# A converted weight's sign as a 16-bit half on GpSimd, and the decay of the scan's state on VectorE

## The chip, the cores and the metric

One Trainium2 chip, one core of it. The metric is the device time of one execution in microseconds (us). Engines are named as in the profile: PE is TensorE's matmul and PEld its weight load, DVE is VectorE, ACT is ScalarE, POOL is GpSimd, SP is SyncE, which issues nearly all the DMAs here. Every engine has its own queue and takes its instructions in order: an instruction that waits for a semaphore holds up all that stand behind it on that engine.

## The reference, cut to what matters

A recurrent attention over 768 steps for 4 batches of 8 heads (head size 40) gives 3072 rows of 320, and two feed-forward blocks follow.

```
for t in range(S):
    y[:, :, t] = einsum('bhd,bhde->bhe', rt, state)
    Sa = einsum('bhde,bhe->bhd', state, at)
    state = state * wt[:, :, None, :] - einsum('bhd,bhe->bhde', Sa, bt) \
            + einsum('bhd,bhe->bhde', vt, kt)
h = x @ w_in;  x1 = (max(h, 0) + alpha * min(h, 0)) @ w_out      # d_ff 2048
g = x1 @ w_gate;  out = (silu(g) * (x1 @ w_val)) @ w_out         # d_ff 1536
```

The weights of both feed-forward blocks lie in memory as 64-bit floats and have to be made 32-bit floats by the kernel itself.

## The kernel before, in words

**The scan.** The steps are worked in chunks of 64, two chunks to an item, and 24 items (six blocks of 128 steps, m = 0 to 5, times 4 batches). `preps` makes the decay products of an item by scans on DVE and scales its inputs; `inverse(m)` inverts the 64 x 64 triangular systems of the whole block m by a chain of some 100 small DVE operations (a product into `tmp`, L645, and a subtraction from `la`, L653, for 31 columns), then two block transposes (L656, L658), from which PE takes the block `eps` (L666); `seq` runs an item's two chunks one after the other: `zp` (PE, L749), `zs` (ACT), `pp` (PE), `ut` (ACT), transposes of `ut` and of the state (PE, L767 and L771), `gp` (PE), the mask (DVE, L785), `yp` (PE), the sum into the state `ST` (DVE, L805) and the output `pv` (DVE, L809). Between two chunks `enter_chunk` multiplies the state by its decay three times: for the two halves of the next chunk's operand `gs` (DVE, 64 x 160 each, L726), and in place for the whole state (POOL, 128 x 160, the same line). POOL also copies `v` into the other halves of `gs` (L740) and makes the triangular selections of `AN` (L598).

**The weights.** `conv1` turns the 32 tiles (128 x 384 and 128 x 320 by turns) of the first block's two matrices into pairs of 32-bit parts, a rounded one and the rest, and writes them to memory as `wd`, from where the first block's matmuls fetch them again (`wt`). Of a 64-bit weight, `narrow` makes a 32-bit one in four passes: ACT scales the upper word, which leaves exponent and upper mantissa in `wz` (L191); ACT brings the upper 16 bits of the lower word to their place in `wy` (L192); DVE puts the sign bit of the upper word into `wy` (L193); DVE shifts `wz` by 3 and joins `wy` (L194). Then ACT rounds (`wc`, L218) and POOL subtracts (`wc`, L219). There are two buffers of `raw`, `wz` and `wc` and one of `wy`. The second block's weights go another way, `gated`, which the change leaves alone; its POOL comparison of one input (L213) serves below as a price.

**The order.** The program is written in generators that `drive` interleaves by shares and priorities, and a list scheduler of the compiler orders each engine's instructions from that. So a changed line moves other instructions too. `inverse(0)` runs beside the first weight tiles; `seq` of block 0, the preparation of block 1 and `inverse(1)` run beside the rest of them; from then on the first feed-forward block's matmuls of block m run beside the scan of block m + 1. The last part is the second feed-forward block alone.

Of the kernel before, what the change touches and what calls it, by code (L numbers as in the profile page):

```python
# [10 lines left out]
U16 = mybir.dt.uint16  # L11
ACTF = mybir.ActivationFunctionType
ALU = mybir.AluOpType
# [60 lines left out]
def kernel(  # L74
# [15 lines left out]
    nc = tc.nc  # L90
# [94 lines left out]
    def narrow(pool, raw):  # L185
        whi, wlo = raw[..., 1], raw.bitcast(U16)[..., 1]
        sh = list(whi.shape)
        y = pool.tile(sh, U32, tag="wy", name="wy", bufs=YB)
        z = pool.tile(sh, U32, tag="wz", name="wz", bufs=ZB)
        f = z.bitcast(F32)  # L190
        nc.scalar.activation(out=f, in_=whi.bitcast(F32), func=ACTF.Copy, scale=2.0 ** -112)  # L191
        nc.scalar.activation(out=y, in_=wlo, func=ACTF.Copy, scale=2.0 ** -13, bias=2.0 ** -14 - 0.5)  # L192
        nc.vector.scalar_tensor_tensor(y, whi, 0x80000000, y, ALU.bitwise_and, ALU.bitwise_or)  # L193
        nc.vector.scalar_tensor_tensor(z, z, 3, y, ALU.logical_shift_left, ALU.bitwise_or)  # L194
        return f

# [24 lines left out]
    def conv(stage, idx, src, f, kind, into=None, dve=0):  # L221
        sw = words(src)
        if kind == "up":
            raw = stage.tile([128, 3, 128, 2], U32, tag="raw", name="raw", bufs=RB)
            sw = sw[:, f * 128:f * 128 + 128]
            nc.sync.dma_start(out=raw[:, 0:2], in_=sw[0:256].rearrange("(j p) n two -> p j n two", p=128))
            for p in (lo, hi):
                nc.sync.dma_start(out=raw[p, 2], in_=sw[256:DM])
        else:
            raw = stage.tile([128, DM, 2], U32, tag="raw", name="raw", bufs=RB)  # L230
            nc.sync.dma_start(out=raw, in_=sw[f * 128:f * 128 + 128])
        w32 = narrow(stage, raw) if idx < 2 * K1 else gated(stage, raw, dve)
        t = stage.tile([128, 768], F32R, tag="wc", name="wc", bufs=WCB) if into is None else into
        if kind == "up":
            t3 = t.rearrange("p (a b) -> p a b", a=6)
            split(w32, t3[:, 0:3], t3[:, 3:6], nc.gpsimd)
        elif kind == "down":
            split(w32[:, 0:256], t[:, 0:256], t[:, 256:512], nc.gpsimd)
            split(w32[:, 256:DM], t[:, 512:512 + RT], t[:, 512 + RT:2 * DM], nc.gpsimd)
        else:  # L240
            split(w32, t[:, 0:DM], t[:, DM:2 * DM], nc.gpsimd)
        if into is None:
            n = 768 if kind == "up" else 2 * DM
            nc.sync.dma_start(out=wd[idx, :, 0:n], in_=t[:, 0:n].bitcast(F32))
# [186 lines left out]
    raw = {}  # L431
    for j, pool in ((0, rawp), (1, bp)):
        for nm in ("w", "bk"):
            sh = [128, 2, NP, TB] if nm == "bk" else [128, 1, NP, TB]
# [267 lines left out]
    def seq(i, ch, own=None):  # L702
# [19 lines left out]
        std = st[:, :, 0:D].rearrange("q (a j) d -> q a j d", j=2)  # L722

        def decayed(eng, out, pr, c):
            wc = wv_all[pr, :, :, c, L:L + 1].to_broadcast([pr.stop - pr.start, NP // 2, 2, D])
            eng.tensor_tensor(out=out, in0=std[pr], in1=wc, op=ALU.mult)  # L726

        def enter_chunk(c):
            t = gs_p.tile([128, NP, 2, L + D], F32, tag="gs", name="gs")
            for h, pr in ((0, lo), (1, hi)):  # L730
                decayed(nc.vector, t[pr, h::2, :, L:L + D], pr, c)
            decayed(nc.gpsimd, std, slice(0, 128), c)
            return t

        nxt = enter_chunk(0)
        for c in range(CPB):
            cs = slice(c * L, c * L + L)
            gs = nxt
            for h, pr in ((0, hi), (1, lo)):
                nc.gpsimd.tensor_copy(  # L740
                    out=gs[pr, h::2, :, L:L + D],
                    in_=rv.rearrange("t (q j d) -> t q j d", j=2, d=D)[(lo, hi)[c], h::2],
# [11 lines left out]
            for q in range(NP):  # L754
                for j, pr in ((0, lo), (1, hi)):
                    u = q // 2 * 2 + j
                    n = bb * NSEG + slots[u][1] * CPB + c
# [14 lines left out]
            for h, pr in ((0, lo), (1, hi)):  # L772
                nc.scalar.mul(
                    out=gs[pr, h::2, :, L:L + D],
                    in_=pp[pr, 1].rearrange("p (a j) d -> p a j d", j=2)[:, :, :, 0:D], mul=-1.0,
# [5 lines left out]
            for q in range(NP):  # L781
# [4 lines left out]
                out=gs[:, :, :, 0:L].rearrange("q p h t -> q (p h) t"),  # L786
# [5 lines left out]
            for u, p in slots:  # L792
                s = p * CPB + c
                u0, j = u // 2 * 2, u % 2
# [11 lines left out]
            if c < CPB - 1:  # L806
                nxt = enter_chunk(c + 1)
            wv = wv_all[:, :, :, c, :]
            nc.vector.tensor_tensor(  # L809
                out=xo.rearrange("q (j a) c t -> q a j c t", j=2)[:, :, :, c],  # L810
# [303 lines left out]
```

## Time and profile before

| | us |
|---|---|
| median of 3 runs (1230.62 to 1232.87) | 1231.44 |
| the profiled execution | 1229.82 |
| its span | 1228.1 |
| PE busy | 1095.4 (89%) |
| PEld busy | 934.2 (76%) |
| DVE busy | 759.5 (62%) |
| ACT busy | 602.0 (49%) |
| POOL busy | 287.4 (23%) |

The profiled execution stands 1.62 us under the median of the runs, and its span 1.7 us under its own time. The shares are averages over unlike stages: in the last 350 us DVE and ACT are idle for most of the time and POOL altogether, while in the first 220 us DVE is the engine that is hardly ever idle. "Granted clock" is TensorE's clock as a share of full speed (2.4 GHz), averaged over a stretch.

### The profile page before, as it was taken

What the parts mean: (1) busy time and instruction counts of PE and PEld (TensorE: products, weight loads), DVE (VectorE), ACT (ScalarE), POOL (GpSimd) and SP (SyncE); (2) the same over time, 40 slices, a digit from 0 to 9 for tenths busy, and PEclk for the clock granted to TensorE, in tenths of its full rate; (3) what the DMA queues carried; (4) which work ended last, traced back from release to release, by engine and by line L of the source; (5) the groups of instructions that cost most, each with busy time, mean ns of one, the idle gap of its engine ahead of it and who ended that gap; (6) DMA issues with size and microseconds to landing.
All of it is one profiled execution on the core that took longest, in us unless ns stands there. A gap on an engine that the chain in (4) does not pass through costs nothing. (4 is left out here: it accounts for less than half of the span.)

```text
span 1228.1 us, 24433 instructions
## 1 busy us (share of the span) xinstructions
PE 1095.4 (89%) x9056; PEld 934.2 (76%) x9056; DVE 759.5 (62%) x1624; ACT 602.0 (49%) x1495; POOL 287.4 (23%) x452
## 2 busy tenths in 40 slices
PE   4146687999999898899989999999999999999998
PEld 4145577877878787788777787787788888888887
DVE  7798988598589669949865434879522323223222
ACT  5559568655954665675655433545332323222222
POOL 8335433401212230341354000536300000000000
PEclk9669776988999998999999999999999999999999
DMA  5534688565554534645486464795010101010000
GB/s 146 186 133 147 214 271 288 172 193 171 158 156 135 175 114 145 194 153 154 125 280 210 148 206 138 250 353 164 1 48 1 48 1 48 1 37 13 22 1 22
DMA packets 94885, 166.36 MB, mean 135 GB/s; under 512 B 13232, under 2 KB 43184, under 8 KB 94768
## 3 DMA queue, kind: packets, MB, share of 16 engines
q1 hardware_dynamic: 86608, 160.88, 41.2%
q10 hardware_dynamic: 8160, 3.93, 1.1%
q8 instruction: 72, 1.18, 0.4%
q14 instruction: 45, 0.37, 0.1%
HBM read 136.98 MB, written 27.79 MB: 134 GB/s over the span
## 5 line engine op out<-in xcount | busy, mean ns | idle before, releaser
L218 ACT CAST gh<-g 128x512 fp32r<-128x512 f32 (+1 forms) x176 | 105.5, 600 | 162.8 <-DVE g L1050 116.2
L1050 DVE TENSOR_TENSOR g<-pv,sg 128x512 f32<-128x512 f32 x72 | 49.7, 691 | 206.3 <-PE pv L274 201.3
L219 DVE TENSOR_TENSOR gl<-g,gh 128x512 fp32r<-128x512 f32 (+1 forms) x176 | 121.9, 692 | 85.7 <-ACT gh L218 83.0
L274 PE MATMUL u<-xh,wt 128*128 128x512 f32 (+1 forms) x416 | 149.0, 401 | 13.5 <-DVE g L315 11.2
L315 DVE SCALAR_TENSOR_TENSOR g<-g,neg,u 128x512 f32<-128x512 f32 (+1 forms) x104 | 73.0, 703 | 88.9 <-ACT g L314 88.4
L274 PEld LDWEIGHTS u<-xh,wt 128*128 128x128 f32 x416 | 80.1, 196 | 32.7 <-DVE g L315 14.4
L314 ACT ACTIVATE g<-u 128x512 f32<-128x512 f32 (+1 forms) x104 | 58.6, 564 | 90.4 <-PE u L274 86.1
L274 PE MATMUL pg<-xh,w 128*128 128x512 f32 x288 | 102.6, 394 | 0.3 <-ACT sg L1048 0.3
L1048 ACT ACTIVATE sg<-pg 128x512 f32<-128x512 f32 x72 | 43.0, 598 | 120.6 <-PE pg L274 120.6
L274 PE MATMUL pv<-xh,w 128*128 128x512 f32 x288 | 100.5, 390 | 0.0
L1034 PE MATMUL o<-w,gh 128*128 128x320 f32 x288 | 87.5, 310 | 2.6 <-ACT gh L218 2.6
L1035 PE MATMUL o<-w,gh 128*128 128x320 f32 x288 | 87.8, 309 | 0.0
L281 PE MATMUL d<-gl,wt 128*128 128x512 f32 (+1 forms) x208 | 82.3, 398 | 1.2 <-DVE gl L219 1.2
L740 POOL COPY gs<-raw_v 64x160 f32<-64x160 f32 x96 | 40.8, 425 | 177.3 <-PE yp L797 108.6
L274 PE MATMUL u<-xl,wt 128*128 128x512 f32 (+1 forms) x208 | 80.8, 389 | 0.0
L653 DVE TENSOR_TENSOR la<-la,tmp 128x96 f32<-128x96 f32 (+43 forms) x306 | 79.3, 285 | 2.0
L282 PE MATMUL d<-gh,wt 128*128 128x512 f32 (+1 forms) x208 | 80.1, 387 | 0.0
L645 DVE TENSOR_TENSOR tmp<-la 128x96 f32<-128x96 f32 (+43 forms) x306 | 78.1, 279 | 1.8
L584 PE MATMUL mnp<-AN,kbt 128*128 128x128 f32 x384 | 59.6, 305 | 21.6 <-DVE AN L559 15.2
L598 POOL TENSOR_SCALAR_AFFINE_SELECT AN<-AN 64x256 f32<-64x256 f32 x96 | 52.2, 544 | 111.2 <-ACT AN L597 99.0
L1036 PE MATMUL o<-w,gl 128*128 128x320 f32 x288 | 77.2, 311 | 1.0 <-DVE gl L219 0.9
L280 PE MATMUL d<-gh,wt 128*128 128x512 f32 (+1 forms) x208 | 72.6, 402 | 2.8 <-DMA wt<-wd 2.8
(123 smaller groups left out, 2635.3 us busy)
## 6 DMA issues: line engine op xcount, KB each, us to landing
wt<-wd SPq DMA_DIRECT2D x98, 384.0 KB
wt<-wd SPq DMA_DIRECT2D x98, 320.0 KB
wd<-wc SPq DMA_DIRECT2D x24, 384.0 KB
raw<-in_moe_w_out_dram SPq DMA_DIRECT2D x28, 320.0 KB
raw_bk<-in_bk_dram SPq DMA_DIRECT2D x48, 160.0 KB
wd<-wc SPq DMA_DIRECT2D x20, 320.0 KB
raw<-in_moe_w_in_dram SPq DMA_DIRECT2D x16, 256.0 KB
raw_v<-in_v_dram SPq DMA_DIRECT2D x24, 160.0 KB
```

The source lines that it names most:

```text
L218: nc.scalar.copy(out=h, in_=raw)
L219: eng.tensor_tensor(out=l, in0=raw, in1=h.bitcast(F32), op=ALU.subtract)
L274: last = nc.tensor.matmul(ps, lt, rh, start=(i == 0), stop=(i == len(ops) - 1))
L280: nc.tensor.matmul(ps, wh, gh, start=first, stop=False)
L281: nc.tensor.matmul(ps, wh, gl, start=False, stop=False)
L282: nc.tensor.matmul(ps, wl, gh, start=False, stop=last)
L315: nc.vector.scalar_tensor_tensor(g, g, neg[:, f:f + 1], ps, ALU.mult, ALU.add)
L645: nc.vector.tensor_tensor(out=tv, in0=ml[:, kk + 1:HALF, kk:kk + 1].to_broadcast([128, nr, ns]), in1=tl[:, kk:kk + 1, c0:c0 + ns].to_broad ...
L653: mark["inv"] = nc.vector.tensor_tensor(out=dst, in0=dst, in1=tv, op=ALU.subtract)
L1034: nc.tensor.matmul(ops[q], gh[:, ts], wh, start=first, stop=False)
L1035: nc.tensor.matmul(ops[q], gh[:, ts], wl, start=False, stop=False)
L1036: nc.tensor.matmul(ops[q], gl[:, ts], wh, start=False, stop=last)
```

## The change

The sign is no longer joined by DVE into the whole 32-bit `wy`. `wy` is seen as pairs of 16-bit halves. POOL compares the topmost 16 bits of the 64-bit weight with 32768 and multiplies by 32768, which gives the sign bit, and writes it as the upper half (now L194); ACT writes its 16 bits into the lower half alone (now L195); DVE's last pass is as it was (now L196). And the in-place decay of the state, 48 operations of 128 x 160, goes from POOL to DVE (now L728). All later lines have numbers that are higher by 2 in the changed kernel.

```diff
@@ narrow
         nc.scalar.activation(out=f, in_=whi.bitcast(F32), func=ACTF.Copy, scale=2.0 ** -112)
-        nc.scalar.activation(out=y, in_=wlo, func=ACTF.Copy, scale=2.0 ** -13, bias=2.0 ** -14 - 0.5)
-        nc.vector.scalar_tensor_tensor(y, whi, 0x80000000, y, ALU.bitwise_and, ALU.bitwise_or)
+        nd = len(sh)
+        y16 = y.bitcast(U16).rearrange("p (n two) -> p n two" if nd == 2 else "p j (n two) -> p j n two", two=2)
+        nc.gpsimd.tensor_scalar(y16[..., 1], raw.bitcast(U16)[..., 3], 32768.0, 32768.0, ALU.is_ge, ALU.mult)
+        nc.scalar.activation(out=y16[..., 0], in_=wlo, func=ACTF.Copy, scale=2.0 ** -13, bias=2.0 ** -14 - 0.5)
         nc.vector.scalar_tensor_tensor(z, z, 3, y, ALU.logical_shift_left, ALU.bitwise_or)
@@ enter_chunk
-            decayed(nc.gpsimd, std, slice(0, 128), c)
+            decayed(nc.vector, std, slice(0, 128), c)
```

Three places of the new order are spoken of below. The first is DVE at the start of `inverse(0)`, between its products (`tmp`) and subtractions (`la`). Before:

```order
L653 TENSOR_TENSOR la<-la,tmp 128x29x3
L653 TENSOR_TENSOR la<-la,tmp 128x13x3
L193 SCALAR_TENSOR_TENSOR wy<-raw,wy 128x320
L645 TENSOR_TENSOR tmp<-la 128x112
L645 TENSOR_TENSOR tmp<-la 128x48
L194 SCALAR_TENSOR_TENSOR wz<-wz,wy 128x320
L653 TENSOR_TENSOR la<-la,tmp 128x28x4
```

Now:

```order
L655 TENSOR_TENSOR la<-la,tmp 128x29x3
L655 TENSOR_TENSOR la<-la,tmp 128x13x3
L647 TENSOR_TENSOR tmp<-la 128x112
L196 SCALAR_TENSOR_TENSOR wz<-wz,wy 128x320
L647 TENSOR_TENSOR tmp<-la 128x48
L655 TENSOR_TENSOR la<-la,tmp 128x28x4
```

One DVE pass of the weight tile is left of two, and it waits for ACT's half and POOL's half of `wy`.

The second is POOL in the same stretch, where `wc` is the subtraction of the tile before. Before:

```order
L219 TENSOR_TENSOR wc<-wz,wc 128x384
L219 TENSOR_TENSOR wc<-wz,wc 128x256
L219 TENSOR_TENSOR wc<-wz,wc 128x64
L219 TENSOR_TENSOR wc<-wz,wc 128x384
```

Now:

```order
L194 TENSOR_SCALAR wy<-raw 128x320
L221 TENSOR_TENSOR wc<-wz,wc 128x384
L194 TENSOR_SCALAR wy<-raw 128x384
L221 TENSOR_TENSOR wc<-wz,wc 128x256
L221 TENSOR_TENSOR wc<-wz,wc 128x64
L194 TENSOR_SCALAR wy<-raw 128x320
```

The sign of a tile stands in front of the subtraction of the tile before it, so that the two take turns on POOL.

The third is DVE at the end of a chunk of the first item, where `pv` is the item's output, `rest` belongs to a later item's preparation and `gs` is the next chunk's operand. Before:

```order
L805 TENSOR_TENSOR ST_174<-yp,ST_174 128x4x40
L809 TENSOR_TENSOR pv<-yp,Wx 128x2x2x64
L193 SCALAR_TENSOR_TENSOR wy<-raw,wy 128x384
L726 TENSOR_TENSOR gs<-ST_174,Wx 64x2x2x40 x2
L194 SCALAR_TENSOR_TENSOR wz<-wz,wy 128x384
```

Now:

```order
L807 TENSOR_TENSOR ST_174<-yp,ST_174 128x4x40
L811 TENSOR_TENSOR pv<-yp,Wx 128x2x2x64
L553 RECIPROCAL first<-rest_114 128x8
L728 TENSOR_TENSOR gs<-ST_174,Wx 64x2x2x40 x2
L728 TENSOR_TENSOR ST_174<-ST_174,Wx 128x4x40
L807 TENSOR_TENSOR ST_176<-yp,ST_176 128x4x40
```

The decay in place stands behind the two operands that the next `zp` reads, and in front of the other item's sum.

## Rows read from the trace of the kernel before

**Rows 1.** Windows: busy us of each engine by stretch (start:end), TensorE's granted clock, DMA share, GB/s
```profile
40.00:78.00 38.00, 1.57 (x58) 1.57 (x60) 35.93 (x108) 11.34 (x29) 7.63 (x11) 0.50 0.48 158
78.00:118.00 40.00, 29.39 (x458) 26.39 (x455) 36.84 (x55) 38.34 (x107) 22.93 (x31) 0.88 0.47 148
118.00:190.00 72.00, 51.34 (x616) 44.97 (x614) 64.59 (x188) 43.23 (x128) 28.09 (x46) 0.76 0.74 239
190.00:218.00 28.00, 23.55 (x287) 21.21 (x289) 23.23 (x35) 26.13 (x73) 12.48 (x18) 0.76 0.88 288
218.00:700.00 482.00, 456.10 (x4953) 382.96 (x4950) 355.42 (x879) 285.86 (x781) 129.41 (x237) 0.96 0.54 167
```
**Rows 2.** Waits: who waited for whom, us in total, times, longest
```profile
PE eps L666 <- DVE la L656: 44.9, 2, 39.9
...
PEld zp L749 <- POOL ST L726: 6.2, 10, 1.6
...
DVE wy L193 <- ACT wy L192: 3.9, 6, 1.1
```
**Rows 3.** Timeline of PE where the two inverses end: start, us, what, [idle before <-releaser]
```profile
76.43 3.63 PE L666 MATMUL eps<-la,tt 32*32 32x32 f32 x128 [39.93 <-DVE la L656]
...
186.34 3.62 PE L666 MATMUL eps<-la,tt 32*32 32x32 f32 x128 [4.99 <-DVE la L656]
```
**Rows 4.** Windows of L193 alone: length, DVE busy (count), then clock and DMA
```profile
40.00:78.00 38.00, 3.09 (x6) 0.50 0.48 158
78.00:118.00 40.00, 5.05 (x6) 0.88 0.47 148
118.00:190.00 72.00, 8.18 (x14) 0.76 0.74 239
190.00:218.00 28.00, 4.74 (x6) 0.76 0.88 288
```
**Rows 5.** Groups of instructions, DVE, 0 to 220 us: busy us, mean ns, idle before
```profile
L193 DVE SCALAR_TENSOR_TENSOR wy<-raw,wy 128x320 uint32<-128x320 uint32 x16 | 12.0, 753 | 2.5 <-ACT wy L192 2.4
...
L194 DVE SCALAR_TENSOR_TENSOR wz<-wz,wy 128x384 uint32<-128x384 uint32 x16 | 9.0, 560 | 0.1
L194 DVE SCALAR_TENSOR_TENSOR wz<-wz,wy 128x320 uint32<-128x320 uint32 x16 | 7.9, 496 | 0.4
```
**Rows 6.** Line L192, ns min/median/max, first and last start
```profile
L192 ACT ACTIVATE wy<-raw x32: 482/517/577, 41.8 to 216.2; 128x384 uint32<-128x384 uint16 x16, 128x320 uint32<-128x320 uint16 x16
```
**Rows 7.** Line L213, POOL's comparison with a constant, ns min/median/max
```profile
L213 POOL TENSOR_SCALAR wz<-wz x24: 1000/1172/1538, 510.1 to 869.8; 128x384 f32<-128x384 f32 x16, 128x320 f32<-128x320 f32 x8
```
**Rows 8.** Timeline of DVE: three places
```profile
42.77 0.55 DVE L193 SCALAR_TENSOR_TENSOR wy<-raw,wy 128x384 uint32<-128x384 uint32 x1
...
44.41 0.36 DVE L645 TENSOR_TENSOR tmp<-la 128x87 f32<-128x87 f32 x2
44.69 1.19 DVE L653 TENSOR_TENSOR la<-la,tmp 128x87 f32<-128x87 f32 x2
...
60.61 0.48 DVE L193 SCALAR_TENSOR_TENSOR wy<-raw,wy 128x320 uint32<-128x320 uint32 x1
...
841.88 0.69 DVE L219 TENSOR_TENSOR xl<-xa,xh 128x512 fp32r<-128x512 f32 x1 [0.21 <-ACT xh L218]
```
**Rows 9.** Timeline of POOL: what ran beside those, and a selection
```profile
44.68 0.99 POOL L219 TENSOR_TENSOR wc<-wz,wc 128x384 fp32r<-128x384 f32 x1 [2.79 <-ACT wc L218]
...
84.52 1.82 POOL L598 TENSOR_SCALAR_AFFINE_SELECT AN<-AN 64x256 f32<-64x256 f32 x2 [3.24 <-ACT AN L597]
...
841.23 1.31 POOL L213 TENSOR_SCALAR wz<-wz 128x320 f32<-128x320 f32 x1
```
**Rows 10.** Line L598, the selection, ns min/median/max
```profile
L598 POOL TENSOR_SCALAR_AFFINE_SELECT AN<-AN x96: 407/413/1449, 18.5 to 553.9; 64x256 f32<-64x256 f32 x96
```
**Rows 11.** Tile ST, the state: its sum and its decay, ns min/median/max
```profile
L726 POOL TENSOR_TENSOR ST<-ST,Wx x48: 451/462/1445, 21.2 to 685.4; 128x160 f32<-128x160 f32 x48
L805 DVE TENSOR_TENSOR ST<-yp,ST x48: 277/320/327, 108.9 to 703.3; 128x160 f32<-128x160 f32 x48
```
**Rows 12.** Windows of L726 alone: length, DVE busy (count), POOL busy (count)
```profile
218.00:700.00 482.00, 27.69 (x76) 19.47 (x38) 0.96 0.54 167
```

## The prediction

> **What bounds the kernel now.** I read the windows first, because the shares of the whole span mislead. After 218 us PE is busy 456.1 of 482 us (95%) and DVE 355.4 (74%): there the matmuls set the time. Before that it is the other way round [rows 1]: from 40 to 78 us PE works 1.6 us of 38 and DVE 35.9; from 78 to 190 us DVE is busy 101.4 of 112 us (91%) and PE 80.7 (72%); only from 190 to 218 us do PE (84%), DVE (83%) and the DMA (0.88) stand close together. So time is to be had in the first 218 us, and from DVE.
>
> The waits say where it is taken up: PE waits for DVE's block transpose at the end of the inverse, 39.9 us at one go the first time [rows 2]. The timeline of PE gives the two gates: `eps` of block 0 starts at 76.43 us after an idle 39.93, `eps` of block 1 at 186.34 after 4.99 [rows 3]. Whatever shortens DVE's queue ahead of these moves both. Around the first gate the granted clock is 0.50 [rows 1]; I count nothing for it, since PE hardly works there.
>
> **Edit 1, the sign: what goes.** 32 passes of L193 go, 6 before 78 us, 6 up to 118, 14 up to 190 and 6 after [rows 4]. The groups give 753 ns for the narrow form against 496 ns for its twin L194 on the same shape [rows 5]; the excess is time in which DVE stood behind POOL (below), and that stall will hit another DVE instruction instead. So I price a pass by the twin: 9.0 + 7.9 = 16.9 us for 32, or 0.53 us each.
>
> **What comes.** POOL gets 32 comparisons with a constant. The trace has no such operation on 16-bit halves; the nearest row is L213, 1.00 to 1.54 us on 32-bit data, median 1.17 [rows 7], and I take 1.2, so 38 us. POOL is busy 71 us of the 178 from 40 to 218 us [rows 1], so it has the room. ACT's pass stays at 0.52 us [rows 6]: as many elements, into half the bytes. No DMA is added. The raw tile is now let go by ACT and POOL and not by DVE, so a next load on SP can be asked for sooner, which I price at nothing: the conversion's pace is not the gate. DVE waited 3.9 us for ACT's half of `wy` [rows 2]; it will wait for POOL's half in the same place. Bounds: nothing, and the 0.8 us a tile of the late-sign rival; I take the old 3.9, since the two ACT passes of a tile last 1.04 us (twice 0.52, [rows 6]), nearly as long as the sign beside them, and tiles follow each other every 3.57 us (60.61 less 42.77 over 5, [rows 8]), so this cancels. Behind a waiting sign stand POOL's subtraction, the selections and the copies of `v` that `zp` needs; the sign waits for the tile's load and for the only `wy` buffer, both of which the old chain also waited for.
>
> **Does POOL's read hold up DVE?** It can: a subtraction at 44.68 us, 0.99 us long [rows 9], lies on a DVE pair that takes 1.19 us where its sister on the same shape took 0.36 [rows 8]. That operation has two inputs. The comparison has one, and inside one of 1.31 us at 841.23 us [rows 9] a DVE instruction with two SBUF inputs takes its 0.69 us undisturbed [rows 8]. A selection, one input too, is itself stretched, 1.82 us for two [rows 9] against 0.41 each [rows 10]. So I charge DVE nothing for the sign, and POOL perhaps half a microsecond more for it.
>
> The Trainium skill (SBUF — State Buffer, section "Who interferes with whom") says that a VectorE instruction with two SBUF inputs and a GpSimd instruction that reads SBUF exclude each other for the whole instruction, whichever starts second. By that the sign would hold DVE up as the subtraction does, and the sum would turn into that of the blocking rival. The subtraction agrees with the sentence; the comparison at 841 us does not.
>
> **Edit 2, the decay.** 48 operations go from POOL, 0.46 us each, to DVE, where the state's sum on the same 128 x 160 takes 0.32 [rows 11]. Ten lie before 218 us (48 less the 38 of [rows 12]): 3.2 us. After it 38 x 0.32 = 12.2 us join a DVE that is 74% busy beside a PE at 95% [rows 1]. Cover: PE has the other block's matmuls to run. If that cover were gone, all 12.2 would be on the path; I take 1 us, about the 5% of the time that PE is idle there. What is gained: `zp` waited 6.2 us in ten places for POOL, with the decay in front of the copies [rows 2]. In the new order it stands behind the operands that `zp` reads, so this wait should go; but DVE's next sum is then late by 0.32, so I count 0 of 6.2.
>
> **The sum.** To the first gate: 6 x 0.53 = 3.2, less two early decays (0.6), gives 2.6 us, and DVE is the only bound there. To the second: 20 x 0.53 = 10.6 less 8 x 0.32 = 2.6 gives 8.0, times DVE's 0.91, so 7.3. Beyond it nothing, since DMA and PE are close there. So the second gate moves up by at most 9.9 us. How much of that reaches the end is the weakest number: the same bytes and matmuls have to pass in less time (DMA 0.74 from 118 to 190 us, 0.88 after, [rows 1]). I take the middle of 2.6 and 9.9, 6.2 us. With 1 us back later, -5.2: 1229.82 - 5.2 = 1224.6 for an execution like the profiled one, and 1.62 more at the median of the runs, **1226.2**.
>
> **The rivals.**
> *No difference.* The early microseconds are taken by the DMA or by the scan's own ping-pong between PE and ACT, and the later ones are hidden. For it: DVE is idle 9% between the gates, DMA is at 0.88 behind them. Against it: 39.9 us of pure waiting for DVE. Time 1231.4, within 2.5 us.
> *Slower, late sign: DVE waits for it in place.* The last pass stands in DVE's order between links of the inverse, so what it waits stops the inverse. Sign 1.2, stretched by 0.5 under DVE, behind half a subtraction 0.5, makes 2.2 us against ACT's 1.04, so up to 1.1 late; I price 0.8. It decides from about 0.4 us a tile: 26 tiles x (0.53 - 0.4) is the 3.2 that the early decays cost. At 0.8: 26 x 0.27 + 3.2 = 10.2 to the second gate, 9.2 by DVE's share, 2.2 to the first; middle 5.7, and 1 later: 1231.44 + 6.7 = 1238.1. Against it: 3.57 us between tiles.
> *Slower, blocking: POOL's read of one input holds DVE up.* 0.83 us each (1.19 - 0.36, [rows 8]): 26 x 0.30 + 3.2 = 11.0 to the second gate, 2.4 to the first, middle 6.7, and 1 later: 1239.1. Against it: the undisturbed 0.69.
> *Slower, decays: they lie on the scan's chain after 218 us.* 12.2 - 6.2 = +6.0: 1237.4. For it: DVE in order, with the inverses of blocks 2 to 5 in its queue. Against it: PE's idle time there is only 5%.
> That the change does not do what it says would mean that ACT's half waits for POOL's half of the same `wy`; the new order has ACT's pass without such a wait on the tile's own sign, so it gets no chance of its own.
>
> **How the numbers follow.** Forecast 0.57 (own range 1219 to 1229), no difference 0.20, late sign 0.12, decays 0.06, blocking 0.05. A measurement here tells 0.2% (2.5 us) from no change; below 1229.0 is faster: 0.57, within 0.20, slower 0.23. Low end: 9.9 + 6.2 (the `zp` waits) = 16.1 off gives 1215.3, hardly all of it, so 1217; high end 1238 takes in most of the three slower cases.
>
> **What would show it.** Right: 32 POOL instructions of 1.0 to 1.7 us on `wy`; DVE waiting for them less than 6 us in all; `eps` of block 0 near 74 us and of block 1 near 177 to 181; 48 DVE decays of about 0.32 us; the POOL wait of `zp` gone. Wrong: DVE waits on POOL's `wy` of over 12 us, small inverse operations of 1 us and more beside a sign, the second gate at 186 or later, or PE idle for more than 30 us from 218 to 700.

## The result, and the profile after

| | before | changed |
|---|---|---|
| median of 4 runs, us | 1231.03 (1230.26 to 1232.87) | 1245.22 (1240.61 to 1249.67) |
| profiled execution, us | 1229.82 | 1242.28 |
| its span, us | 1228.1 | 1240.6 |

The changed kernel is slower: the ratio is 1.0114, 95% interval 1.0081 to 1.0147, some 14 us. The forecast was 1226.2.

The page of the changed kernel, its first lines (span; busy time of each engine):

```profile
span 1240.6 us, 24428 instructions
## 1 busy us (share of the span) xinstructions
PE 1098.4 (89%) x9056; PEld 932.9 (75%) x9056; DVE 756.4 (61%) x1640; ACT 604.5 (49%) x1495; POOL 312.8 (25%) x436
```

The windows of the changed kernel over the same stretches as [rows 1]:

```profile
40.00:78.00 38.00, 1.12 (x42) 1.12 (x44) 34.41 (x101) 12.53 (x32) 18.61 (x19) 0.54 0.52 168
78.00:118.00 40.00, 30.30 (x440) 26.65 (x436) 34.34 (x50) 36.23 (x98) 31.67 (x32) 0.80 0.47 149
118.00:190.00 72.00, 49.87 (x508) 43.34 (x507) 61.69 (x175) 43.30 (x132) 49.27 (x59) 0.74 0.72 226
190.00:218.00 28.00, 20.04 (x364) 18.25 (x363) 21.19 (x29) 23.81 (x62) 17.54 (x16) 0.76 0.80 249
218.00:700.00 482.00, 449.13 (x4861) 374.81 (x4859) 354.94 (x908) 284.69 (x775) 111.79 (x200) 0.97 0.56 167
```

From 40 to 218 us DVE has 151.6 us of work where it had 160.6, and POOL 117.1 where it had 71.1. The relief of DVE is there, and it is smaller than POOL's new load. PE did not gain by it: 101.3 us busy in that stretch, 105.9 before. And from 218 to 700 us, where not one sign is left, PE is idle 32.9 us instead of 25.9.

The two gates, in PE's timeline of the changed kernel, as [rows 3]:

```profile
76.88 3.62 PE L668 MATMUL eps<-la,tt 32*32 32x32 f32 x128 [39.02 <-DVE la L658]
...
190.79 2.49 PE L668 MATMUL eps<-la,tt 32*32 32x32 f32 x128
```

They stood at 76.43 and 186.34: the second is 4.5 us later, where 177 to 181 was forecast. The groups of POOL up to 218 us (busy us, mean ns, idle before and what ended it) tell what the sign costs there:

```profile
L194 POOL TENSOR_SCALAR wy<-raw 128x384 uint16<-128x384 uint16 (+1 forms) x32 | 59.0, 1844 | 30.5 <-DVE wz L196 11.5 <-DVE pv L811 4.4 <-DMA raw<-in_moe_w_in_dram 3.2
L221 POOL TENSOR_TENSOR wc<-wz,wc 128x384 fp32r<-128x384 f32 (+2 forms) x46 | 36.0, 793 | 8.8 <-ACT wc L220 7.8 <-DVE gs L787 0.7
L600 POOL TENSOR_SCALAR_AFFINE_SELECT AN<-AN 64x256 f32<-64x256 f32 x35 | 21.3, 609 | 15.1 <-ACT AN L599 11.2 <-POOL wy L194 0.9 <-POOL wc L221 0.9
```

It is 59.0 us, not 38. Its line by itself (ns min/median/max), then ACT's half and the decay:

```profile
L194 POOL TENSOR_SCALAR wy<-raw x32: 1382/1636/4422, 40.4 to 211.7; 128x384 uint16<-128x384 uint16 x16, 128x320 uint16<-128x320 uint16 x16
```
```profile
L195 ACT ACTIVATE wy<-raw x32: 551/596/660, 43.1 to 213.7; 128x384 uint16<-128x384 uint16 x16, 128x320 uint16<-128x320 uint16 x16
```
```profile
L728 DVE TENSOR_TENSOR ST<-ST,Wx x48: 296/318/1134, 23.4 to 706.6; 128x160 f32<-128x160 f32 x48
```

And the waits of DVE for the two halves of `wy` (us, times, longest):

```profile
DVE wz L196 <- POOL wy L194: 4.3, 3, 1.6
DVE wz L196 <- ACT wy L195: 3.3, 2, 1.7
```

So DVE hardly waits for the sign in place, 4.3 us in three places. The delay must have another way to the second gate.

### Where block 1's inversion starts

The second gate is the end of `inverse(1)`. Its first product reads two scratch tiles, both named `la`: DVE fills one by a transpose (L630, now L632), and POOL prepares the other by two operations (`MEMSET la`: 128 x 1024 zeros, then 128 x 32 ones; "the clearing" below). POOL's timeline of the kernel before:

```profile
116.79 0.95 POOL L632 MEMSET la<- 128x1024 f32 x1
117.81 0.89 POOL L598 TENSOR_SCALAR_AFFINE_SELECT AN<-AN 64x256 f32<-64x256 f32 x2
118.65 0.16 POOL L633 MEMSET la<- 128x32 f32 x1
```

and of the changed kernel:

```profile
118.71 1.09 POOL L600 TENSOR_SCALAR_AFFINE_SELECT AN<-AN 64x256 f32<-64x256 f32 x2
119.78 1.38 POOL L194 TENSOR_SCALAR wy<-raw 128x320 uint16<-128x320 uint16 x1
121.11 0.99 POOL L221 TENSOR_TENSOR wc<-wz,wc 128x384 fp32r<-128x384 f32 x1
122.05 0.95 POOL L634 MEMSET la<- 128x1024 f32 x1
123.07 1.17 POOL L600 TENSOR_SCALAR_AFFINE_SELECT AN<-AN 64x256 f32<-64x256 f32 x2
124.22 1.64 POOL L194 TENSOR_SCALAR wy<-raw 128x384 uint16<-128x384 uint16 x1
125.80 1.00 POOL L221 TENSOR_TENSOR wc<-wz,wc 128x256 fp32r<-128x256 f32 x2
126.74 0.16 POOL L635 MEMSET la<- 128x32 f32 x1
```

The second clearing comes at 126.74 instead of 118.65. Between the first clearing and the second there was one pair of selections; now a sign and two subtractions stand there too, and the first clearing is itself late by the signs before it. DVE's timeline of the changed kernel at the same place:

```profile
121.61 1.95 DVE L632 STREAM_TRANSPOSE la<-tt 128x1024 f32<-128x1024 f32 x1 [2.11 <-ACT tt L595]
123.48 0.49 DVE L196 SCALAR_TENSOR_TENSOR wz<-wz,wy 128x320 uint32<-128x320 uint32 x1
126.25 0.96 DVE L196 SCALAR_TENSOR_TENSOR wz<-wz,wy 128x384 uint32<-128x384 uint32 x1 [2.29 <-ACT wz L191]
129.17 0.69 DVE L787 TENSOR_TENSOR gs<-gp,mask 128x512 f32<-128x512 f32 x1 [1.96 <-PE gp L784]
129.78 0.29 DVE L647 TENSOR_TENSOR tmp<-la 128x31 f32<-128x31 f32 x2
```

In the kernel before it read:

```profile
116.45 2.01 DVE L630 STREAM_TRANSPOSE la<-tt 128x1024 f32<-128x1024 f32 x1
118.37 0.67 DVE L194 SCALAR_TENSOR_TENSOR wz<-wz,wy 128x320 uint32<-128x320 uint32 x1
118.96 0.29 DVE L645 TENSOR_TENSOR tmp<-la 128x31 f32<-128x31 f32 x2
```

The first product runs at 129.78; before it ran at 118.96. The clearing had landed at 126.90, 8.1 us later than before. The other 2.7 us are DVE's own order: a mask pass (L787) stands in front of the product, and it waited for PE's `gp`. So it is in five of the seven kernels below that have all signs and the clearing on POOL; in the two others the clearing itself let the product go, as here with the sign alone:

```profile
126.10 0.53 DVE L647 TENSOR_TENSOR tmp<-la 128x31 f32<-128x31 f32 x2 [0.31 <-POOL la L635]
```

From the first product to the end of the products (the start of the first block transpose) it takes 188.58 - 129.78 = 58.8 us, before 184.22 - 118.96 = 65.3. In that stretch 13 sign passes (7.7 us) stood on DVE before and none now, and six decays (2.0 us) came in. So the inversion is 6.5 us shorter, and it starts 10.8 us later. That is the 4.4 us by which it ends later.

### The profile page after: what moved, and what is told of

Same layout as the page of the kernel before. It is cut to its first block, busy times and chain, and to the rows that moved or that the text cites. A ratio compares the mean times of both kernels' runs of the same rounds, so it can differ in the third digit from the quotient of the medians.

```text
span 1240.6 us, 24428 instructions
## 1 busy us (share of the span) xinstructions
PE 1098.4 (89%) x9056; PEld 932.9 (75%) x9056; DVE 756.4 (61%) x1640; ACT 604.5 (49%) x1495; POOL 312.8 (25%) x436
## 4 chain that ended last, share of the span: by engine, by line
PE 49%; DMA 5%; DVE 5%; ACT 3%; issue 2%; SPq 1%; POOL 1%; ACTq 0%; DVEq 0%; POOLq 0%
PE pg L276 10%; PE pv L276 9%; PE u L276 8%; PE o L1038 3%; PE o L1037 3%; PE o L1036 3%; PE d L284 2%; PE d L283 2%; PE d L282 2%; PE gp L784 1%; DMA raw<-in_moe_w_gate_dram 1%; PE yp L799 1%; PE d L288 1%; PE mnp L586 1%; DMA raw<-in_moe_w_val_dram 1%
## 5 line engine op out<-in xcount | busy, mean ns | idle before, releaser
L1050 ACT ACTIVATE sg<-pg 128x512 f32<-128x512 f32 x72 | 43.1, 598 | 121.7 <-PE pg L276 121.6
L655 DVE TENSOR_TENSOR la<-la,tmp 128x96 f32<-128x96 f32 (+43 forms) x306 | 83.0, 297 | 2.1
L284 PE MATMUL d<-gh,wt 128*128 128x512 f32 (+1 forms) x208 | 80.0, 386 | 0.0
L600 POOL TENSOR_SCALAR_AFFINE_SELECT AN<-AN 64x256 f32<-64x256 f32 x96 | 47.9, 499 | 120.6 <-ACT AN L599 110.9
L586 PEld LDWEIGHTS mnp<-AN,kbt 128*128 128x128 f32 x384 | 55.0, 219 | 26.0 <-DVE AN L561 13.5
```

The costliest lines, as they stand in the source:

```text
L284: nc.tensor.matmul(ps, wl, gh, start=False, stop=last)
L586: nc.tensor.matmul(ps[:, s].rearrange("p h t -> p (h t)"), kbt[:, g * SH + s].rearrange("p j t -> p (j t)"), an[:, :, g * SH + s, :],)
L655: mark["inv"] = nc.vector.tensor_tensor(out=dst, in0=dst, in1=tv, op=ALU.subtract)
```

## Experiments

Eighteen kernels were run, each three rounds against the kernel before. The table gives the ratio with its interval, the first product of `inverse(1)`, the second gate and the last state sum (us, from each profile). "None" has neither edit, "both" is the changed kernel. Draws are explained under the second heading below.

| edits | draw | ratio | first product | gate 2 | last sum |
|---|---|---|---|---|---|
| none | as is | 1 | 119.0 | 186.3 | 703.3 |
| none | halves | 0.9935 (0.9912 to 0.9958) | 121.0 | 185.0 | 704.7 |
| none | priority | 0.9978 (0.9961 to 0.9995) | 120.7 | 188.1 | 708.5 |
| none | ACT swap | 1.0047 (1.0029 to 1.0066) | 121.6 | 188.5 | 710.0 |
| sign | as is | 1.0006 (0.9985 to 1.0027) | 126.1 | 185.3 | 705.7 |
| sign | halves | 0.9951 (0.9930 to 0.9973) | 127.9 | 188.0 | 707.5 |
| sign | priority | 1.0190 (1.0166 to 1.0214) | 129.6 | 186.4 | 713.0 |
| decay | as is | 1.0047 (1.0025 to 1.0069) | 120.6 | 186.7 | 716.6 |
| decay | halves | 0.9958 (0.9939 to 0.9977) | 120.6 | 188.6 | 711.6 |
| decay | priority | 1.0074 (1.0048 to 1.0100) | 119.9 | 185.6 | 717.4 |
| decay | ACT swap | 1.0023 (1.0000 to 1.0047) | 120.6 | 186.5 | 714.8 |
| both | as is | 1.0114 (1.0081 to 1.0147) | 129.8 | 190.8 | 721.6 |
| both | halves | 1.0050 (1.0030 to 1.0069) | 129.1 | 194.1 | 709.1 |
| both | priority | 1.0064 (1.0039 to 1.0089) | 129.5 | 190.9 | 712.1 |
| both | ACT swap | 1.0096 (1.0071 to 1.0121) | 129.6 | 191.5 | 725.0 |
| no sign | as is | 0.9980 (0.9963 to 0.9996) | 119.8 | 176.4 | 709.5 |
| sign late | as is | 0.9960 (0.9934 to 0.9985) | 122.5 | 182.4 | 707.4 |
| sign early | as is | 1.0092 (1.0056 to 1.0127) | 124.6 | 195.0 | 716.6 |
| both, clearing on DVE | as is | 1.0047 (1.0022 to 1.0072) | 124.4 | 180.7 | 701.5 |
| sign, clearing on DVE | halves | 0.9944 (0.9917 to 0.9970) | 124.0 | 179.0 | 703.1 |

The last sum does not order the times: with the halves swapped, decay alone has it at 711.6 and the ratio 0.9958, both edits at 709.1 and 1.0050.

### Each edit alone, and the sign left out

Sign alone is the kernel before with the first hunk of the change, decay alone with the second. In the third run the sign is left out:

```diff
-        nc.vector.scalar_tensor_tensor(y, whi, 0x80000000, y, ALU.bitwise_and, ALU.bitwise_or)
```

> Only the sign on POOL; the decay in place goes back to POOL. Three theories of the 14 us. LOAD (the sign's 52 us on POOL, 1.6 us each, stand ahead of the selections of AN and the subtractions, and delay what the scan waits for): 1242 to 1248, the first state sums still about 6 us late. DECAYS (48 decays of 0.32 us on DVE lie on the scan's chain): 1226 to 1232, and the lateness that arises after 400 us is gone. ORDER (the compiler's scheduler, given other operations, draws another order in which a block's scan starts later; neither part costs much by itself): anything from 1228 to 1248, with the lateness arising at other chunks than in the changed kernel.

Measured 1.0006: the sign alone costs and gives nothing that shows. Its first state sum is 5.7 us late, as LOAD had it, but the time is some 10 us under LOAD's range.

> Only the decay in place on DVE; the sign stays with DVE as it was. LOAD: 1230 to 1233, since POOL carries no sign. DECAYS: 1238 to 1246, with the lateness arising after 218 us at every chunk, some 0.3 us each. ORDER: 1228 to 1240, with jumps at single chunks where the order differs and none in between.

Measured 1.0047, 1236.72 us. That falls into the range of ORDER and just under that of DECAYS, with the lateness of the state sums in jumps: 2 to 6 us up to 260 us, 14 at 474, 4 at 540, 19 at 634, 13 at the last sum. At the end of the same profiled execution (1230.85) only 1.0 us of it is left.

> The kernel before without the sign pass on DVE: the sign bit of the converted weights is left out of the computation. It is the most that any way of taking the sign off DVE can give. LOAD and DECAYS: the 16.9 us of DVE are really gone and nothing is added, so 1219 to 1227, with the second gate at 172 to 180 us. ORDER: the gates come earlier by some us, but the end can lie anywhere from 1222 to 1238; if it is not under 1229, the DVE pass was worth nothing to begin with.

The gate is in the range expected, 176.36, ten microseconds earlier, and the time is 1228.91, ratio 0.9980, above the range that LOAD and DECAYS gave and inside that of ORDER. So 32 passes off DVE with nothing put in their place are worth 0.2%, 2.5 us. That is well under 6.2.

### Draws: the same work in another order

The order of each engine's instructions comes from the compiler's scheduler, and an edit can make it draw again. Three edits that give no engine more or less work were laid on the kernels. "ACT swap" writes the two ACT passes of a weight tile in the other order, "halves" the two products of `enter_chunk`, "priority" raises the scan of block 0:

```diff
-            for h, pr in ((0, lo), (1, hi)):
+            for h, pr in ((1, hi), (0, lo)):
                 decayed(nc.vector, t[pr, h::2, :, L:L + D], pr, c)
...
-    SP = 3000
+    SP = 4000
```

> The kernel before with the two ACT passes of a weight tile written in the other order: the same instructions on the same engines. LOAD and DECAYS: no difference, 1229 to 1233. ORDER: the time moves by 3 us or more in either direction, which then is the size of what the scheduler alone does to an edit that changes no engine's work.

Measured 1.0047: a neutral edit costs as much as the decay alone.

> The kernel before with one neutral edit: the two halves of the next chunk's operand are multiplied by their decay in the other order. No engine has more or less to do. ORDER: another draw of the scheduler's order, so 1226 to 1240 like the swapped ACT passes, which came out 0.47% slower. LOAD and DECAYS: 1229 to 1233, and then the swapped ACT passes were slower for a cause of their own.

Measured 0.9935, 1223.30 us: another neutral edit gives 0.65%. LOAD and DECAYS both said 1229 to 1233. This kernel is faster than both kernels of this case, and its windows show by how little such a draw differs (the last two stretches of [rows 1]):

```profile
190.00:218.00 28.00, 21.07 (x248) 19.33 (x247) 20.40 (x32) 22.84 (x66) 11.29 (x13) 0.70 0.73 237
218.00:700.00 482.00, 457.07 (x5016) 381.75 (x5017) 359.29 (x889) 291.98 (x793) 137.84 (x242) 0.98 0.56 172
```

PE is busy 1.0 us more from 218 to 700 us, at a granted clock of 0.98 instead of 0.96.

> The changed kernel with the same neutral edit (halves in the other order). ORDER: if the 14 us are mostly the draw, this one comes back by 4 us or more, to 1230 to 1241. If the change itself costs them (sign and decays together, since each alone gave 0.06% and 0.47%), it stays at 1242 to 1248.

Measured 1237.19, 1.0050: it comes back by 8 us, as ORDER has it, yet it stays 1.15% above the kernel before with the same edit.

> Only the decay in place on DVE, with the halves in the other order. DECAYS (48 times 0.33 us on DVE stand in front of what the scan waits for): 1235 to 1240 again, as in the run with the decay alone (0.47% slower). ORDER: 1228 to 1240, and the mean over the three draws with the decay on DVE is no more than 2 us above the mean over the draws with it on POOL.

> Only the decay in place on DVE, with the two ACT passes of a weight tile in the other order. DECAYS: 5 to 6 us above the kernel before with the same swap, so 1241 to 1246. ORDER: anything from 1228 to 1242, not the sum of the two.

Measured 0.9958 and 1.0023: neither the 1235 to 1240 of DECAYS nor its sum of two (1241 to 1246). The first, 1225.62 us, lies under ORDER's range too. The fourth pair came later:

> Only the decay in place on DVE, with the higher priority for the scan of block 0, which gave 0.9978 of before with the decay on POOL. DECAYS: 1.002 or more, in every pair above its partner. ORDER: anywhere from 0.994 to 1.012, and the mean of the pairs within 0.4% of nothing.

Measured 1.0074, so 0.96% above its partner. The four pairs of decay alone against none are +0.47, +0.23, +0.96 and -0.24%, mean +0.36%. Whether the decays cost anything isn't settled: the draws scatter by more than that.

> Only the sign on POOL, with the halves of the next chunk's operand in the other order; that edit took 0.65% off the kernel before, 0.64% off the changed one and 0.89% off the one with the decay alone. SIGN (the sign on POOL costs as much as it saves, within 0.3%, and the rest is order): 0.992 to 0.997 of before, so 1221 to 1227. LOAD (POOL's 50 us delay the scan, and the run with the sign alone had a lucky order): 1230 to 1240.

> The kernel before with a higher priority for the scan of block 0 (4000, was 3000): the third draw of an order with no work moved between engines. ORDER: anything from 1222 to 1240. If the delay at the start (the first state sum 6 us late in the changed kernel) is what costs, this one starts its scan earlier and ends at 1225 to 1231.

> Only the sign on POOL, with the higher priority for the scan of block 0. SIGN (it gives and takes about the same): within 0.4% of the kernel before at the same priority. LOAD: 0.6 to 1.2% above that one.

Measured 0.9951, 0.9978 and 1.0190. The first two fit SIGN. The third does not: the slowest kernel of all, 2.1% above its partner, beyond the range that LOAD gave. Its gate is at 186.4, in its place, and by the count of matmul columns done its PE is 2.7 us late where the kernel before stands at 250 us, 4.9 at 350, 14.2 at 450 and 26.9 at 725; most of the time goes from 350 us on, where it has no sign. Its three longest idle times of PE there are 4.3 us at 360 us, 5.9 at 412 and 6.0 at 726. So this too looks like a draw, the worst one; no run here shows what in it costs the time.

> The changed kernel with the higher priority for the scan of block 0. PAIR (sign and decay together cost 1.1%, as in the two pairs measured so far, 1.14% and 1.15%, though neither does alone): 0.9 to 1.3% above the kernel before at the same priority. ORDER (each is a draw of its own from a range of some 20 us): 1228 to 1242, without regard to the kernel before at that priority.

Measured 1.0064, 0.86% above the partner at 0.9978: a hair under PAIR's 0.9 to 1.3, and inside ORDER's range too.

> The changed kernel with the two ACT passes written ahead of the sign: PE's and DVE's instructions come in just the same order as in the changed kernel, and only ACT and POOL take a few in other turns. ORDER: the time stays at that of the changed kernel, 1241 to 1249, though the same swap took the kernel before up by 0.47% where it redrew PE's and DVE's order. If it moves by more than 5 us, PE's and DVE's order alone does not set the time.

Measured 1245.26 (1245.23 to 1245.58), ratio 1.0096, where the changed kernel had 1245.22 (1240.61 to 1249.67) and 1.0114. It is nearly the same program: in the two traces PE and POOL run the same sequence of operations, DVE's differs in 2 places of 1640 and ACT's in 18 of 1495. So this row is hardly a draw of its own; where the same swap redrew PE's and DVE's order, it cost 0.47%.

Laid side by side by draw, the whole change stands above its partner by +1.14, +1.15, +0.86 and +0.49%, in every draw and by +0.91% in the mean. The sign alone stands above it by +0.06, +0.16 and +2.12%.

### What the signs delay

The sign was put on POOL for a part of the tiles only; `idx` is the tile's number, and the other condition was `7 <= idx < 13`:

```diff
-    def narrow(pool, raw):
+    def narrow(pool, raw, idx):
...
+        if idx >= 13:
+            nc.gpsimd.tensor_scalar(y16[..., 1], raw.bitcast(U16)[..., 3], 32768.0, 32768.0, ALU.is_ge, ALU.mult)
...
+        else:
...
+            nc.vector.scalar_tensor_tensor(y, whi, 0x80000000, y, ALU.bitwise_and, ALU.bitwise_or)
```

> The sign on POOL for tiles 13 to 31 only, which are converted after the selections of AN for block 1 are done; tiles 0 to 12 keep it on DVE, and the decay stays on POOL. GATE (signs ahead of the selections delay the start of inverse(1): its first product stood at 119.0 to 121.6 us without them and at 126.1 to 129.8 with them): first product at 119 to 122, second gate at 176 to 181 as where the sign is left out (176.4), against 185.3 with all signs on POOL. If DVE waits for POOL's half in any case, the gate stays at 184 or later. In time 0.994 to 1.004 of before, by the draw of the order.

> The mirror: the sign on POOL for tiles 7 to 12 only, which are converted beside the selections for block 1; all others keep it on DVE. GATE: the delay without the gain, first product at 124 to 129 and the second gate at 190 to 195. If POOL's turns at the selections do not matter, first product at 119 to 122 and the gate at 184 to 187. In time 0.996 to 1.008 of before, by the draw of the order.

The gates of the late and the early form, in PE's timelines:

```profile
182.39 3.63 PE L672 MATMUL eps<-la,tt 32*32 32x32 f32 x128
```
```profile
194.98 3.62 PE L672 MATMUL eps<-la,tt 32*32 32x32 f32 x128 [9.12 <-DVE la L662]
```

The late form, 19 signs on POOL, has its gate at 182.39 (1.4 us above what GATE allowed, with the first product 0.5 us above) and a ratio of 0.9960. The early form puts six signs on POOL and has its gate at 194.98 and a ratio of 1.0092, just above its range and nearly that of the whole change. Six signs at the wrong place can cost what 32 do. Of the 8.6 us by which its gate is late, 5.7 stand at the first product; the inversion itself takes 3.0 us more than before, and no run shows why.

Last, the two clearings of `la` for block 1 went to DVE:

```diff
-        nc.gpsimd.memset(tl, 0.0)
-        nc.gpsimd.memset(tl.rearrange("p a b -> p (a b)")[:, 0:HALF * HALF:HALF + 1], 1.0)
+        (nc.vector if m == 1 else nc.gpsimd).memset(tl, 0.0)
+        (nc.vector if m == 1 else nc.gpsimd).memset(tl.rearrange("p a b -> p (a b)")[:, 0:HALF * HALF:HALF + 1], 1.0)
```

> The changed kernel, with the two clearings of la for block 1 (128 x 1024 and 128 x 32) on DVE, not POOL. On POOL the second stood at 126.6 to 128.9 us behind 8 or 9 signs, against 118.6 to 121.4 without signs. GATE: the transpose of la stays at 121 to 123 us (it waits for the selections' results), so the first product comes to 124 to 126, from 129.8, and the second gate to 184 to 187, from 190.8. If POOL's clearing is not what the first product waits for, it stays at 129 or later. In time, by the draw of the order, 0.996 to 1.010 of before; under 1.005 would fit that a gate at 190 or later is what all five kernels that were 0.5 to 1.1% slower share with it.

DVE's timeline of that kernel:

```profile
120.97 1.94 DVE L632 STREAM_TRANSPOSE la<-tt 128x1024 f32<-128x1024 f32 x1 [2.10 <-ACT tt L595]
123.08 0.91 DVE L634 MEMSET la<- 128x1024 f32 x1 [0.17 <-issue]
123.90 0.43 DVE L196 SCALAR_TENSOR_TENSOR wz<-wz,wy 128x320 uint32<-128x320 uint32 x1
124.31 0.09 DVE L635 MEMSET la<- 128x32 f32 x1
124.44 0.63 DVE L647 TENSOR_TENSOR tmp<-la 128x31 f32<-128x31 f32 x2
```

The first product runs at 124.44, as expected, right behind the clearing, and the gate stands at 180.67, better than the 184 to 187 expected. Of the 10.8 us by which the inversion started late, 5.3 went with the clearing and with DVE's order behind it, for the mask pass now stands behind the product; the other 5.5 come with the transpose, which waits for ACT's copies into `tt` (L595) and stands at 120.97, 4.5 us after the 116.45 of the kernel before. Why these copies are later (the last at 121.3 in the changed kernel, 115.8 before) is not shown: no row has them waiting for POOL. The gate moved by 10.1 us and the first product by 5.3, because the inversion also takes 54.0 us instead of 58.8, with fewer passes of the scan and of the first feed-forward block in it. The time is 1.0047 instead of 1.0114, more than half of the loss, if that is not again the draw: DVE's order changed with the move.

> The sign alone on POOL, the halves in the other order (0.9951 of before), and the two clearings of la for block 1 on DVE. GATE: first product at 122 to 125 (127.9 without the move), second gate at 180 to 184 (188.0). In time 0.990 to 1.000 of before; the kernel before with the halves in the other order stands at 0.9935.

Measured 0.9944, gate 178.99, where the same kernel without the move had 0.9951 and 187.97. Here nine microseconds at the gate are worth nothing that shows.

## Why the prediction was wrong

**The sign's price, too low.** 32 x 1.2 = 38 us were taken from 32-bit comparisons [rows 7]; it measured 59.0, median 1.64, with four above 2.4 us. ACT's half pass was to stay at 0.52 and takes 0.60.

**The step that failed: "so it has the room".** POOL was idle for 107 of 178 us [rows 1], and from that average came "nothing" for the signs' effect on anything but DVE's own wait. The prediction even named what would stand behind a sign, the subtraction, the selections and the copies of `v`, but put no price on it, and left out the clearing of `la`, which `inverse(1)` needs. From 78 to 118 us POOL was already busy 22.9 of 40 us. With eight or nine signs there (17 to 19 us; the changed kernel's first four there last 3.41, 2.56, 2.38 and 2.55), POOL works without a gap of 0.1 us from 111.73 to the end of the clearing at 126.90, and the first product comes at 126.1 to 129.8 in all seven kernels with all signs and the clearing on POOL, against 119.0 to 121.6 in the nine with no sign there. The late form has none in that stretch and 122.5, the early one six and 124.6. That the place on POOL moves the gate is shown by runs: signs only after the selections, gate 182.4; signs only beside them, 195.0; the clearing away from POOL, 180.7. The selections themselves are not shown to hold the inversion up; by the kernel it reads `tt` and the clearing, not their results.

**What the passes on DVE are worth at the gate: right.** "At most 9.9 us" was worked out; where the sign is left out the second gate moved up 10.0 us. That it fits so closely is in part luck, since the neutral edits alone move that gate by -1.4 to +2.2 us. In the changed kernel the inversion is indeed 6.5 us shorter. The gain was made and given back at the start.

**What a gate is worth: mis-sized.** The middle, 6.2 of 9.9, was called the weakest number. Ten microseconds gave 0.2% where the sign is left out, and nine gave nothing in the pair with the clearing on DVE. A later gate is another matter: the five kernels whose second gate is at 190.8 or later are all slower, by 0.50 to 1.14%, mean 0.83%; the fifteen with a gate at 188.6 or earlier lie between -0.65 and +1.90%, mean +0.1%. Four of the five carry both edits, and two of them are nearly the same program, so this alone shows little. The two late gates that were moved by experiment agree (+0.92% for the early signs; 0.67% back for the clearing), each in one draw. The matmul columns that PE has done, counted in each profiled execution, agree for these three: where the kernel before stands at 218 us the changed kernel is 7.2 us late and the early form 8.3, while the changed kernel with the clearing on DVE is 2.4 us ahead. But the sign alone, with its gate in its place, is 6.4 us late there and 2.2 at the end, and without the sign PE is 4.7 us late in spite of its early gate and 0.6 at the end. So the gate is not all that sets it, and such a delay can be made up; why the one stays and the other does not was not tried.

**First gate.** 74 forecast, 76.88 measured. Where the sign is left out it is 73.61, 2.8 us earlier, as 6 x 0.53 = 3.2 has it; with the sign alone 75.25. In the changed kernel `inverse(0)` starts late, its transpose at 42.49 instead of 40.58, and DVE stood 3.54 us for ACT's copy of `tt` in front of it (3.14 before), so the two early decays, priced at 0.6, are not what held it there.

**The decay.** The number of the decays, 48, and their duration, 0.318 us, were right, and the wait of `zp` for POOL's decay [rows 2] is gone from the changed kernel. What took its place: "PEld zp <- issue", 12.5 us in 32 places against 5.6 in 21. The +1 us for the late ones was not confirmed: the pairs say +0.36% in the mean, from -0.24 to +0.96, so anything from nothing to the rival's 6 us and more is possible.

**The order, which the prediction had no term for.** After 218 us the two kernels do the same work except for the 38 decays, and PE still loses time there. Counted by the columns of the matmuls in PE's timeline, the changed kernel is 6.0 us late where the kernel before stands at 250 us, 6.7 at 450, 3.5 at 550, 10.2 at 600, and 12.2 at 725, where 47.3% of them are done. So about half of the lateness is there behind the second gate, and the rest arises far from any sign. One place in that stretch, in windows of the changed kernel:

```profile
582.00:589.00 7.00, 4.28 (x56) 3.40 (x55) 5.94 (x18) 5.86 (x19) 0.00 (x0) 0.75 0.53 162
589.00:596.00 7.00, 7.00 (x34) 5.89 (x33) 4.45 (x18) 3.12 (x9) 0.00 (x0) 0.76 0.22 67
596.00:603.00 7.00, 5.17 (x89) 4.57 (x88) 6.88 (x27) 2.90 (x7) 1.41 (x4) 0.97 0.68 190
603.00:610.00 7.00, 7.00 (x38) 5.10 (x38) 4.75 (x17) 3.07 (x10) 0.00 (x0) 0.79 0.18 57
```

and in the kernel before, in the same windows:

```profile
582.00:589.00 7.00, 6.74 (x66) 5.03 (x62) 6.89 (x25) 1.79 (x3) 1.88 (x5) 1.00 0.42 131
589.00:596.00 7.00, 4.49 (x76) 3.53 (x76) 5.61 (x21) 5.13 (x19) 0.48 (x1) 1.00 0.59 162
596.00:603.00 7.00, 7.00 (x106) 5.67 (x106) 6.50 (x11) 1.89 (x4) 0.62 (x2) 1.00 0.24 78
603.00:610.00 7.00, 7.00 (x274) 6.32 (x269) 4.96 (x13) 6.80 (x13) 5.37 (x8) 1.00 0.32 81
```

The last column but two is the granted clock, a mean over its two levels (1.2 and 2.4 GHz). PE stood still for 2.2 us from 583.7, waiting for `zs` of the scan, and the clock is 0.75 and 0.76 in that window and the next; after 1.8 us of idling between 596 and 603 it is 0.79. The kernel before idled 2.5 us between 589 and 596 and kept 1.00, so the idle time of one window alone does not decide it. Over the whole stretch from 218 to 700 us the clock is no lower in the changed kernel (0.97, before 0.96); what it has more of is idle time of PE, 7.0 us. How much of that is the draw is not shown for this kernel; the neutral edits size a draw at -0.65 to +0.47% on the kernel before.

**The sum of the change.** Sign alone +0.06%, decay alone +0.47%, the late gate of both 0.67% (taken back by the clearing on DVE) add up to 1.20%, beside the 1.14% measured. That they meet is luck as much as proof. Each carries a draw; the parts do not add up elsewhere (with the higher priority sign alone is +2.12%, decay alone +0.96% and both +0.86%), and with the sign alone and the halves swapped the same move of the clearing gave 0.07%. What is sure is that the change is slower in all four draws; how the 14 us divide stays open.

**The rivals.** Late sign fell: DVE waited 4.3 us for POOL's half, under the 6 that were to show it absent, though the time came out beyond its 1238. Blocking has nothing for it in the rows: beside the longest sign DVE's pairs keep their time (last section). Decays on the scan's chain stays open, as said. "No difference" was wrong for the change, but describes the sign alone in two of its three draws. The mechanism that moved the second gate stood in none of them: an engine with room on average, in whose queue the clearing for the next block stands behind the new work. Of what was to show the forecast wrong, two did: the second gate at 186 or later, and PE idle over 30 us from 218 to 700 us.

## What to carry to other kernels

An engine's idle share does not say that it has room: ask at which place of its queue the new instructions stand, and what behind them somebody waits for; here two clearings of 0.95 and 0.16 us behind eight signs came 8.1 us later, and the next block's inversion with them. Where a scheduler orders the program, lay two or three neutral edits on the kernel before believing a difference under 1%: here they alone moved the time from -0.65 to +0.47%, and the best kernel of the study, 0.9935, is one of them. And work taken off a busy engine is worth what the next bound lets through: ten microseconds at the gate became two and a half.

## What had not been expected of the hardware

A sign can be stretched to more than twice its time while DVE beside it loses none. In the changed kernel POOL's timeline has one of 4.42 us, where the median is 1.64:

```profile
144.16 4.42 POOL L194 TENSOR_SCALAR wy<-raw 128x384 uint16<-128x384 uint16 x1 [2.29 <-DVE wz L196]
```

Beside it DVE works off its chain of products and subtractions (first and last pair shown), and then waits:

```profile
144.17 0.53 DVE L647 TENSOR_TENSOR tmp<-la 128x192 f32<-128x192 f32 x2
...
146.52 0.57 DVE L655 TENSOR_TENSOR la<-la,tmp 128x220 f32<-128x220 f32 x2
148.61 1.04 DVE L196 SCALAR_TENSOR_TENSOR wz<-wz,wy 128x384 uint32<-128x384 uint32 x1 [1.52 <-POOL wy L194]
```

The pairs take 0.53 to 0.57 us, as the same shapes do in the kernel before with POOL idle beside them (0.53 at 135.58, 0.57 at 138.80). DVE's run ends at 147.09, the sign 1.49 us later, about the time that a sign takes by itself; DVE then stood 1.52 us for it. The kernel before has the same without a sign: at 139.74 us two subtractions on POOL (128 x 256 and 128 x 64), 1.32 us at 119.56, last 3.71 us beside a run of DVE without a gap. It is not so every time: the sign at 51.82 us, beside DVE pairs of the same kind, took 1.42. What tells the two apart was not tried.

The other way round, DVE's pass at 148.61 runs beside a subtraction of POOL, which has two inputs, and takes 1.04 us; passes of that line with nothing on POOL beside them have a median of 0.48, over both widths. The Trainium skill (SBUF — State Buffer, section "Who interferes with whom") has a VectorE instruction with two SBUF inputs and a GpSimd instruction that reads SBUF contend, and the second one to issue wait for the whole of the first. For the stretched pass the trace agrees that the two meet; at the long sign it was POOL that gave way, over a run of many VectorE instructions and not one.
